# Four staging buffers for weight gradients, and a new order and new buffer addresses, in a gated S4-plus-MLP forward and backward kernel

## The chip, the cores and the metric

The kernel runs on one core of one Trainium2 chip, in one launch. The metric is device time in microseconds (us), the median of several runs. Inputs and all outputs are bf16.

## The reference

A gate mixes two branches; the kernel computes the result and the gradients with respect to everything but the MLP's own input `x`, which is the same array as `u` and is not differentiated as such. L = 2048 rows, D = 448 channels, N = 256 states, F = 1792 hidden units.

```python
g = sigmoid((u * gate_w).sum(-1, keepdims=True))
# branch a: a state-space layer, as a long convolution through FFTs of length 2L
dt = exp(log_dt); A, B, C complex of D x N
K = einsum("dn,dnl,dn->dl", C, exp(dt*A*l), dt*B).real      # l = 0..L-1
a = irfft(rfft(pad(u)) * rfft(pad(K)))[:L] + u * Dskip
# branch b: an MLP with a squared ReLU
b = relu(x @ w1 + b1)**2 @ w2 + b2
y = g * a + (1 - g) * b
# outputs: y, and vjp(grad_out) for u, A, B, C (real and imaginary parts),
# log_dt, Dskip, w1, b1, w2, b2, gate_w       -> 15 outputs
```

## The kernel before

**How the program is made.** `build()` (from L618) records 2757 tasks: a matmul group with its shared bank, a vector or scalar operation, a DMA. A task has an engine and often an alternative (a cast on ACT or DVE, a DMA issued by SP or POOL). Nothing is scheduled when the kernel is built: `replay` (L448) reads two tables of numbers. `ORDER` (L461) holds every task once, as its number times four plus the number of the alternative taken, in the order in which instructions are emitted; so it sets each engine's queue and which engine takes which task. `HOMES` (L580) gives the address of each of 808 buffers in one SBUF area, the "arena", of 106,368 bf16 elements per partition. Two buffers with one address take turns, and the later one's writer waits for the earlier one's last reader. Each engine runs its own queue in order; a DMA's issue instruction, too, waits at the head of its issuer's queue until its data and its target are free. All instructions are emitted in one loop, so the profile's lines tell only the kind: L1585 matmul, L1587 transpose on TensorE, L1589 transposing DMA, L1593 activation, L1595 cast, copy or DMA, L1597 any other element-wise operation. The names `arena` and `banks` stand for all of SBUF and PSUM (8 banks). DRAM scratch keeps its names: `sp` for spectra, `hd` for half-way results of inverse transforms, `br_d` for rows of the MLP branch, `st_d`, `pg_d`, `raw_d` for sums and tables of the parameter gradients, `dh_d` and `r2_d` for hidden activations.

**What it computes, in order of its ranks.**

- Head: loads, the gate, spectra of u and of g times the incoming gradient by two-step transforms (`fwd1` L750, `fwd2` L784) of matmuls with constant tables; the spectra go to `sp`.
- Dense branch: `x @ w1`, squared ReLU and `@ w2` in four blocks of rows, forward and backward. `project` (L975) makes the "dense rows" that the two row outputs need, and they wait in `br_d`. A column of matmuls over 16 row tiles forms each block of the gradient of w2 (L1060) and of w1 (L1270); ACT or DVE casts the bank into a staging buffer `dws`, and a DMA takes it to its output.
- State-space parameters in seven passes (L1134 to L1226): powers, tables, a first half that forms the convolution kernel, and a second half, the gradients, whose sums go to `st_d`.
- Last part (from L1297): the spectrum of the kernel K (`spk`); then, for each of two outputs and four quarters q, a saved spectrum is loaded (`sx`), DVE multiplies it (T1 and T2), `inv1` (L802) does the first step of the inverse transform, casts the banks into a buffer `st` and writes it to `hd` (`hd1` for y, `hd2` for the gradient of u). Then come the outputs' rows (L1374 for y, L1400 for the gradient of u): a quarter loads its part of `hd` (`hs`, 896 KB) and four pieces of dense rows (`brr`, from `br_d`), TensorE adds the dense rows to the second step of the inverse (`inv2` L1342), DVE or ACT moves the result out of the bank into a buffer `ao`, and four DMAs take the rows out.
- Parameter gradients: two groups (passes 0 to 3, then 4 to 6) of element-wise operations of DVE on `st_d`, `pg_d` and `raw_d` (L1434), the sum for log_dt (`dlog`), 36 transposes of 128x128 and 12 of 128x64, and the outputs of A, B and C.

**What holds the rows of one output together.** A load of `hs` reads, on every partition, pieces that all eight groups of `inv1` of that output have written; it waits for all writes of `hd1` (or `hd2`):

```python
d(hd[i], 8 * q * D, [[32 * D, 128], [1, 8 * D]], [("hd", i)])      # load_hs, L820: one key for the whole of hd[i]
```

Each quarter of y then is (L1374):

```python
hs = load_hs(1, q)
br = load_br(0, q)
st = R.buf("ao", 1792)
for hp in range(2):
    py = R.ps("y", 2)
    inv2(hs, hp, q, ..., [(negI..., br...)])
    for x in range(2):
        V("scalar_tensor_tensor", out=jk..., in0=ps..., in1=Gt..., accum_out=dg...)
        V("scalar_tensor_tensor", out=st..., in0=ps..., scalar=gt32..., in1=br...)
rows_out(o0, q, st)
```

The first of the two DVE operations gives the gate's gradient, which the rows of the gradient of u need; so every quarter of y comes ahead of any of the gradient of u.

Of the kernel before, what the change touches and what calls it, by code (L numbers as in the profile page):

```python
# [447 lines left out]
def replay(R, order, homes):  # L448
# [169 lines left out]
def build(nc, R, A_u, Ap, A_log_dt, A_Dskip, B_w1, B_b1, B_w2, B_b2, gate_w, grad_out, outs):  # L618
# [66 lines left out]
    place = {}  # L685
# [177 lines left out]
    for e in range(6):  # L863
        sg = R.buf("dks", 896)
# [193 lines left out]
    dws = [place[f"dws{i}"] for i in range(2)]  # L1058
    nd = 0
    for j in range(FT):  # L1060
# [4 lines left out]
        sg = dws[nd % 2]  # L1065
# [208 lines left out]
    for jg in range(4):  # L1274
# [6 lines left out]
        for dt in range(4):  # L1281
# [4 lines left out]
            sg = dws[nd % 2]  # L1286
# [341 lines left out]
```

## Time and profile before

| | |
|---|---|
| median of 3 runs | 805.7 us (802.41, 805.7, 806.49) |
| the profiled execution | 806.5 us, of which the span of instructions 804.7 us |
| mean granted TensorE clock | 0.904 of full speed |
| matmuls on PE | 11,044 |
| busy: PE, DVE, ACT, POOL | 662.0, 566.1, 476.8, 161.7 us |
| DMA bytes | 138.07 MB, mean 172 GB/s |
| tasks by engine: DVE, ACT, POOL, SP | 831, 713, 270, 164 |

A row of a stretch's table gives its start and end, its length, then for each engine the busy time and the number of instructions, then the granted clock, the mean busy share of the core's 16 DMA engines, and GB/s. A row of waits names the waiting engine and line, what it waited for, the total, how often, and the longest. A row of the timeline has start, length, engine, line, operation, shapes and count, and in brackets how long the engine had stood still before it and what came last. SP has no busy time of its own; it only issues DMAs.

### The profile page before, as it was taken

What the parts mean: (1) busy time and instruction counts of PE and PEld (TensorE: products, weight loads), DVE (VectorE), ACT (ScalarE), POOL (GpSimd) and SP (SyncE); (2) the same over time, 40 slices, a digit from 0 to 9 for tenths busy, and PEclk for the clock granted to TensorE, in tenths of its full rate; (3) what the DMA queues carried; (4) which work ended last, traced back from release to release, by engine and by line L of the source; (5) the groups of instructions that cost most, each with busy time, mean ns of one, the idle gap of its engine ahead of it and who ended that gap; (6) DMA issues with size and microseconds to landing.
All of it is one profiled execution on the core that took longest, in us unless ns stands there. A gap on an engine that the chain in (4) does not pass through costs nothing.

```text
span 804.7 us, 24883 instructions
## 1 busy us (share of the span) xinstructions
PE 662.0 (82%) x11046; PEld 445.2 (55%) x11046; DVE 566.1 (70%) x863; ACT 476.8 (59%) x711; POOL 161.7 (20%) x274
## 2 busy tenths in 40 slices
PE   4587899887999597797779999987698899677477
PEld 4575475556676465465477777765565545542112
DVE  4796766978589658858958895797442665786665
ACT  4999887789687576466555543632226966143125
POOL 6121321202102001210000221022001033332434
PEclk9869999999999899898789999989689999697759
DMA  9846968724206465553424553335942559997996
GB/s 297 253 174 222 339 243 316 197 94 163 73 37 190 150 135 126 126 90 80 136 44 100 185 184 111 101 96 180 174 136 97 108 175 259 236 223 245 263 314 190
DMA packets 112805, 138.07 MB, mean 172 GB/s; under 512 B 75701, under 2 KB 93674, under 8 KB 112058
## 3 DMA queue, kind: packets, MB, share of 16 engines
q0 software_dynamic: 20480, 78.95, 30.1%
q1 hardware_dynamic: 88922, 55.84, 28.5%
q10 hardware_dynamic: 3296, 1.70, 0.9%
q8 instruction: 86, 1.41, 0.7%
q14 instruction: 21, 0.17, 0.1%
HBM read 60.01 MB, written 60.16 MB: 149 GB/s over the span
## 4 chain that ended last, share of the span: by engine, by line
PE 50%; DVE 19%; ACT 10%; DMA 10%; issue 8%; POOL 1%; SPq 0%; ACTq 0%; DVEq 0%; POOLq 0%
PE banks L1585 50%; DVE arena L1597 16%; ACT arena L1595 8%; DVE arena L1595 4%; DMA arena<-br_d 3%; ACT arena L1593 2%; DMA arena<-in_A_u_dram 1%; DMA arena<-c_MI 1%; DMA hd<-arena 1%; DMA arena<-sp 1%; DMA arena<-in_grad_out_dram 1%; DMA out_dram<-arena 1%; DMA arena<-st_d 1%; POOL hd L1595 0%; ACT L1593 0%
## 5 line engine op out<-in xcount | busy, mean ns | idle before, releaser
L1585 PE MATMUL banks<-arena 128*128 128x128 bf16 (+10 forms) x10998 | 658.8, 251 | 138.0 <-ACT arena L1595 45.3
L1585 PEld LDWEIGHTS <-arena 128*32 128x32 bf16 (+6 forms) x10994 | 442.2, 104 | 349.4 <-issue 191.0
L1597 DVE TENSOR_TENSOR arena<-arena 128x256 bf16<-128x256 bf16 (+14 forms) x501 | 384.7, 812 | 66.5 <-ACT arena L1593 30.8
L1595 ACT CAST arena<-banks 128x896 bf16<-128x896 f32 (+6 forms) x411 | 314.1, 828 | 180.1 <-PE banks L1585 137.7
L1595 DVE CAST arena<-banks 128x1024 bf16<-128x1024 f32 (+6 forms) x73 | 75.5, 1048 | 95.4 <-PE banks L1585 92.0
L1593 ACT ACTIVATE arena<-arena 128x256 f32<-128x256 f32 (+8 forms) x138 | 77.5, 586 | 49.7 <-DVE arena L1597 25.0
L1595 POOL DMA_DIRECT2D out_dram<-arena x54 | 29.5, 548 | 170.8 <-ACT arena L1595 130.6
L1597 DVE TENSOR_TENSOR arena<-banks,arena 128x1024 bf16<-128x1024 f32 (+2 forms) x46 | 40.5, 891 | 26.4 <-PE banks L1585 16.6
L1595 ACT COPY arena<-banks 128x168 f32<-128x168 f32 (+3 forms) x36 | 15.3, 438 | 64.9 <-PE banks L1585 64.6
L1597 DVE SCALAR_TENSOR_TENSOR arena<-arena 128x128 f32<-128x128 f32 (+1 forms) x86 | 30.0, 349 | 13.3 <-DMA arena<-in_A_u_dram 9.9
L1595 POOL DMA_DIRECT2D hd<-arena x35 | 22.2, 635 | 61.6 <-ACT arena L1595 51.3
L1595 ACT COPY arena<-arena 128x256 bf16<-128x256 bf16 (+4 forms) x54 | 27.9, 564 | 8.4 <-DVE arena L1597 8.1
L1595 ACT CAST arena<-arena 128x768 bf16<-128x768 f32 (+3 forms) x33 | 26.5, 807 | 9.2 <-DVE arena L1597 9.2
L1597 DVE SCALAR_TENSOR_TENSOR arena<-banks,arena 128x448 bf16<-128x448 f32 x32 | 19.0, 647 | 17.1 <-PE banks L1585 17.1
L1593 ACT ACTIVATE arena<-banks 128x1024 bf16<-128x1024 f32 (+1 forms) x29 | 25.6, 904 | 7.6 <-PE banks L1585 7.4
L1595 POOL DMA_DIRECT2D br_d<-arena x24 | 13.3, 556 | 77.6 <-ACT arena L1595 72.4
L1595 POOL DMA_DIRECT2D st_d<-arena x11 | 6.1, 551 | 90.3 <-ACT arena L1595 90.3
L1595 POOL DMA_DIRECT2D r_d<-arena x14 | 11.6, 829 | 52.1 <-ACT arena L1593 36.3
L1597 DVE TENSOR_SCALAR arena<-arena 128x448 bf16<-128x448 bf16 (+9 forms) x50 | 17.6, 387 | 5.2 <-ACT arena L1593 1.9
L1595 POOL DMA_DIRECT2D dh_d<-arena x7 | 7.8, 1108 | 55.0 <-DVE arena L1597 46.4
L1595 POOL DMA_DIRECT2D arena<-in_grad_out_dram x20 | 12.9, 648 | 14.9 <-PE banks L1585 11.7
L1595 POOL DMA_DIRECT2D arena<-br_d x21 | 11.2, 538 | 3.5 <-DMA hd<-arena 1.9
(48 smaller groups left out, 84.0 us busy)
## 6 DMA issues: line engine op xcount, KB each, us to landing
r_d<-arena POOLq DMA_DIRECT2D x14, 896.0 KB, 5.8
arena<-hd SPq DMA_DIRECT2D x12, 896.0 KB, 13.2
hd<-arena POOLq DMA_DIRECT2D x35, 224.0 KB, 5.1
dh_d<-arena POOLq DMA_DIRECT2D x7, 896.0 KB, 6.0
sp<-arena POOLq DMA_DIRECT2D x6, 896.0 KB, 9.1
arena<-r_d POOLq DMA_DIRECT2D x5, 896.0 KB, 5.1
arena<-sp SPq DMA_DIRECT2D x5, 896.0 KB, 8.7
out_dram<-arena POOLq DMA_DIRECT2D x28, 112.0 KB, 4.2
```

The lines of the kernel that those rows point to most:

```text
L1585: fn(out, **kw)
L1593: fn(out, kw.pop("in_"), kw.pop("func"), **kw)
L1595: fn(out, kw["in_"])
L1597: fn(out=out, **kw)
```

## The change

The code changes in four lines: two staging buffers become four. Everything else is in the two tables, which are new from the first row to the last.

```diff
-                  ("dws0", 512), ("dws1", 512), ("xu1", 1024), ...
+                  *((f"dws{i}", 512) for i in range(4)), ("xu1", 1024), ...
...
-    dws = [place[f"dws{i}"] for i in range(2)]
+    dws = [place[f"dws{i}"] for i in range(4)]
...
-        sg = dws[nd % 2]
+        sg = dws[nd % 4]
...
-            sg = dws[nd % 2]
+            sg = dws[nd % 4]
...
 ORDER = [
-    0, 10, 13, 4, 16, 22, 26, 28, 34, 40, 36, 44, 72, 48, 52, 56, 61, 65, 68, 1724, 1440, 292, 92, 1732,
+    0, 10, 13, 4, 21, 18, 26, 28, 34, 37, 41, 44, 72, 48, 57, 61, 69, 65, 52, 1440, 260, 92, 1732, 1724,
...
```

The tasks, their shapes and their number stay: 2757 tasks, 11,044 matmuls on PE. 307 tasks change their engine, most of them casts that ACT and DVE exchange: DVE has 834 tasks (831 before), ACT 710 (713), POOL 258 (270), SP 176 (164). Of the loads of dense rows, 13 go from POOL's queue to SP's and 5 the other way. By the addresses in `HOMES`, buffers of these names have so many different places:

| buffers | before | after |
|---|---|---|
| staging of weight gradients (`dws`) | 2 | 4 |
| dense rows for the outputs (`brr`, 8 loads) | 6 | 7 |
| rows that leave (`ao`, 8) | 5 | 7 |
| products of spectra (`T1`, 12) | 10 | 11 |
| loaded spectra (`sx`, 8) | 8 | 7 |
| loaded half-way results (`hs`, 8) | 8 | 7 |
| half-way results before they are written (`st`, 24) | 19 | 15 |
| first-step results of forward transforms (`b1`) | 23 | 21 |

Three places where the order differs. First SP's queue in the last part. `arena<-br_d 32x2x896` is one piece of dense rows, `arena<-hd 128x3584` a load of `hs`, `hd<-arena 64x4x448` a write of half-way results, `out_dram<-arena 128x256` an output of the A, B and C gradients, `arena<-sp` a saved spectrum. Before:

```order
L1595 DMA arena<-sp 128x3584
L1595 DMA arena<-hd 128x3584
L1595 DMA out_dram<-arena 128x256
L1595 DMA arena<-hd 128x3584
L1595 DMA arena<-br_d 32x2x896 x2
L1595 DMA arena<-hd 128x3584
L1595 DMA out_dram<-arena 64x256
L1595 DMA out_dram<-arena 128x256
L1595 DMA hd<-arena 64x4x448
L1595 DMA out_dram<-arena 32x2x896 x3
L1595 DMA arena<-br_d 32x2x896 x2
L1595 DMA arena<-hd 128x3584
```

After:

```order
L1595 DMA st_d<-arena 128x256 x2
L1595 DMA hd<-arena 64x4x448
L1595 DMA arena<-br_d 32x2x896 x4
L1595 DMA arena<-st_d 128x1536
L1595 DMA arena<-br_d 32x2x896 x4
L1595 DMA hd<-arena 64x4x448
L1595 DMA arena<-br_d 32x2x896
L1595 DMA hd<-arena 64x4x448
L1595 DMA arena<-hd 128x3584 x3
L1595 DMA out_dram<-arena 128x256 x2
L1595 DMA arena<-hd 128x3584
```

Nine pieces of dense rows and the second group's load of `st_d` now stand ahead of the first load of `hs`; before, loads of `hs` and dense rows alternated and writes of `hd2` stood between them. The first three loads of `hs` now follow the last writes of `hd1`, and the fourth stands behind two outputs.

Second, DVE's queue where the last rows and the second group of parameter gradients meet. `SCALAR_TENSOR_TENSOR 128x448` is an operation of y; `TENSOR_TENSOR 128x384` and `128x3x4x16` are operations of the second group; `COPY 128x768` empties a bank of transposes; the rows of `128x2x2` are the gate's gradient. Before:

```order
L1597 SCALAR_TENSOR_TENSOR arena<-banks,arena 128x448 x16
L1595 CAST arena<-arena 128x2x2 x2
L1597 TENSOR_TENSOR arena<-arena 128x2x2 x2
L1595 CAST arena<-arena 128x2x2 x2
L1597 TENSOR_TENSOR arena<-arena 128x384 x2
L1597 TENSOR_TENSOR arena<-arena 128x3x4x16 x2
L1597 TENSOR_TENSOR arena<-arena 128x384 x3
```

After:

```order
L1597 TENSOR_TENSOR arena<-arena 128x3x4x16
L1597 TENSOR_TENSOR arena<-arena 128x384 x2
L1597 TENSOR_TENSOR arena<-arena 128x3x4x16 x2
L1597 SCALAR_TENSOR_TENSOR arena<-banks,arena 128x448 x2
L1597 TENSOR_TENSOR arena<-arena 128x384
L1597 SCALAR_TENSOR_TENSOR arena<-banks,arena 128x448
L1597 TENSOR_TENSOR arena<-arena 128x384
L1597 SCALAR_TENSOR_TENSOR arena<-banks,arena 128x448
L1597 TENSOR_TENSOR arena<-arena 128x384 x3
L1595 COPY arena<-banks 128x768
L1597 TENSOR_TENSOR arena<-arena 128x384 x2
L1597 SCALAR_TENSOR_TENSOR arena<-banks,arena 128x448 x9
```

Before, the second group began after the last operation of y. Now most of the group (27 operations) stands ahead of the first operation of y, the rest of it between them, and 9 operations of y come last.

Third, ACT's queue at the last blocks of the gradient of w1. `CAST 128x512`, `65x512`, `128x256` are casts into `dws` (512 or 256 columns of w1's gradient); `CAST 128x896` belongs to the inverse transforms, `128x672` to the gradient passes. Before:

```order
L1595 CAST arena<-banks 128x512
L1593 ACTIVATE arena<-arena 128x4x4x16
L1595 CAST arena<-banks 128x896 x4
L1595 CAST arena<-banks 65x512
L1595 CAST arena<-banks 128x256 x2
L1595 CAST arena<-banks 128x896 x8
L1595 CAST arena<-banks 128x256
```

After:

```order
L1595 CAST arena<-banks 65x512
L1595 CAST arena<-banks 128x896
L1595 CAST arena<-banks 128x256
L1595 CAST arena<-banks 128x896 x3
L1595 CAST arena<-banks 128x672 x2
L1595 CAST arena<-banks 128x256
L1595 CAST arena<-banks 128x672
L1595 CAST arena<-banks 128x256
```

The last casts into `dws` come earlier than most of the casts of the inverse transforms, spread between casts of the gradient passes, and each has a buffer that was last used four casts before, not two.

More of the change, by code (lines that the diff above doesn't have):

```diff
@@ L686, in build @@
     for nm, n in (("dKc", 4704), ("dKg0", 672), ("dKg1", 672), ("stg0", 512), ("stg1", 512), ("Z0", 5376), ("Z1", 5376), *((f"YT{i}", 2048) for i in range(NYT)), ("KS", NA * 112), ("KT0", 336), ("KT1", 336),
-                  ("dws0", 512), ("dws1", 512), ("xu1", 1024), ("dnC", 7168), ("xT0", 1024), ("xT1", 1024), ("br0", 448), ("br1", 448),
+                  *((f"dws{i}", 512) for i in range(4)), ("xu1", 1024), ("dnC", 7168), ("xT0", 1024), ("xT1", 1024), ("br0", 448), ("br1", 448),
                   *((f"XP{i}", 5376) for i in range(NXP)), ("Y", 8192), ("X1", 5376), ("Vt", 4096), ("xu0", 1024), ("ry", 2560), ("rx", 3072), ("X0", 5376), ("dnB", FT * D), ("dnA", 7200)):
```

296 rows, old and new, of tables (HOMES, ORDER) are left out of this document.

## The prediction

> **What bounds the kernel now.** I read the profile's page first.
>
> ```profile
> span 804.7 us, 24883 instructions
> PE 662.0 (82%) x11046; PEld 445.2 (55%) x11046; DVE 566.1 (70%) x863; ACT 476.8 (59%) x711; POOL 161.7 (20%) x274
> PE   4587899887999597797779999987698899677477
> PEclk9869999999999899898789999989689999697759
> ```
>
> PE works 662.0 of 804.7 us, so it is the bound on average, and the change leaves its matmuls as they are. What can change is the 142.7 us in which PE stands. Slices of the page show them: the head, then small gaps, then the last six slices, where PE is at 4 to 7 tenths and its clock falls. The table of stretches splits it (columns: start, end, length, busy time and count of PE, PEld, DVE, ACT, POOL, granted clock, share of the DMA engines, GB/s).
>
> ```profile
> 140.00:640.00 500.00, 427.18 (x8678) 307.18 (x8670) 359.56 (x522) 291.89 (x454) 67.08 (x103) 0.92 0.47 125
> 660.00:700.00 40.00, 32.88 (x449) 20.41 (x448) 24.86 (x15) 17.10 (x26) 12.30 (x22) 0.89 0.98 267
> 700.00:740.00 40.00, 29.75 (x223) 16.33 (x222) 32.75 (x39) 13.69 (x19) 11.99 (x20) 0.80 1.01 240
> 740.00:805.00 65.00, 41.23 (x281) 13.49 (x277) 39.63 (x104) 21.42 (x36) 26.93 (x49) 0.74 0.78 239
> 752.70:783.30 30.60, 16.47 (x85) 3.52 (x89) 18.09 (x55) 6.42 (x14) 10.37 (x20) 0.50 0.95 290
> ```
>
> In the long middle PE stands 500 − 427.18 = 72.8 us with the DMA engines half used. After 700 it stands 105 − 29.75 − 41.23 = 34.0 us, and no engine is full there but the DMAs. So I read waits of two stretches, 640 to 805 and 140 to 640 (engine, line, what it waited for, total, times, longest).
>
> ```profile
> PE banks L1585 <- DMA arena<-br_d: 21.9, 5, 9.6
> PE banks L1585 <- ACT arena L1595: 7.9, 3, 5.7
> ACT arena L1595 <- DMA out_dram<-arena: 8.1, 2, 6.6
> ...
> PE banks L1585 <- ACT arena L1595: 22.5, 29, 3.8
> PE banks L1585 <- DVE arena L1597: 21.6, 13, 5.4
> ```
>
> Three rows are the last part, two the middle. The timeline gives the places in the last part.
>
> ```profile
> 725.20 0.37 ACT L1595 CAST arena<-banks 128x256 bf16<-128x256 f32 x1 [6.60 <-DMA out_dram<-arena]
> 725.62 6.65 PE L1585 MATMUL banks<-arena 128*128 128x256 bf16 x44 [5.73 <-ACT arena L1595]
> 736.70 5.65 PE L1585 MATMUL banks<-arena 128*128 128x448 bf16 x29 [4.43 <-DMA arena<-br_d]
> 758.96 3.50 PE L1585 MATMUL banks<-arena 128*128 128x448 bf16 x20 [9.64 <-DMA arena<-br_d]
> 767.60 3.50 PE L1585 MATMUL banks<-arena 128*128 128x448 bf16 x20 [5.14 <-DMA arena<-br_d]
> ```
>
> The first two are one event: ACT may not cast w1's gradient before a staging buffer has been read out, and PE waits for the bank. The other three are quarters of y, and what came last for each is dense rows, not `hs`. The chain that ended last goes through both (start, length):
>
> ```profile
> 717.30 7.74 DMA out_dram<-arena
> ...
> 727.01 9.55 DMA arena<-br_d
> ...
> 749.65 4.71 DMA hd<-arena
> ...
> 756.01 11.46 DMA arena<-br_d
> ...
> 796.68 3.32 PE banks L1585 x4
> 800.07 0.52 ACT arena L1595
> ```
>
> **Part by part.** All sums are made against the profiled execution's own 806.5 us; the median of the runs is 0.8 less, far under the 0.5% (4 us) that a measurement of this kernel can tell from no change.
>
> *Staging.* With four buffers a cast waits for the write-out four casts before. The chain's 7.74 us of write-out at 717.30 goes, and PE's wait of 5.73 with it. Bounds: 0, if the bank was freed late for another reason, and −8.1, all that ACT waits for such writes here. I take −5.7, the row of the place itself. Next late there is DVE's products, which have 32.75 of 40 us busy.
>
> *Dense rows.* In the order before, a piece of `br_d` that a y needs stands on SP behind a load of `hs`, which waits for `hd`; after, nine stand ahead of the first `hs`. The three waits, 4.43 + 9.64 + 5.14 = 19.2, go. Bounds 0 and −21.9 (all five). I take −19.2, since those rows have the order's places.
>
> *A new wait.* In the order after, the last writes of `hd1` stand directly ahead of the first loads of `hs`, and the y that need them follow on PE with little else left: the transforms of the gradient of u are done by then. Rows for that chain, from the last cast of an inverse transform:
>
> ```profile
> L1595 ACT CAST arena<-banks 128x896 bf16<-128x896 f32 x46 | 39.9, 911 | 23.3 <-PE banks L1585 18.6 <-DMA arena<-br_d 2.8 <-DMA out_dram<-arena 1.5
> L1595 POOL DMA_DIRECT2D hd<-arena x27 | 17.0, 633 | 44.8 <-ACT arena L1595 38.5 <-DMA arena<-sp 4.1 <-DMA hd<-arena 1.8
> 651.96 8.21 DMA arena<-sp
> arena<-hd SPq DMA_DIRECT2D x8, 896.0 KB, 13.6
> hd<-arena POOLq DMA_DIRECT2D x27, 224.0 KB, 4.9
> L1587 PE MATMUL banks<-arena 128*128 128x128 bf16 x36 | 2.9, 220 | 0.0
> L1587 PE MATMUL banks<-arena 128*64 128x128 bf16 x12 | 1.0, 223 | 0.0
> ```
>
> Cast 0.9, issue 0.6, write 4.7 (the chain's row), load 8.2 (a load of the same 896 KB that the chain of the stretch from 640 waited for, from `sp`): +14.4. Below: transposes of the parameter gradients fill it, 2.9 + 1.0 = 3.9, so +10.5. Above: write 4.9 and load 13.6, the medians, and the same cast and issue: +20.0. I take 14.4, since nothing else is left to be loaded at that moment if dense rows came earlier. Behind the waiting load on SP stand two outputs and all later `hs`; y's DVE operations and then those of the gradient of u wait for it.
>
> *DVE's second group.* 27 operations of it now stand ahead of the first y on DVE.
>
> ```profile
> L1597 DVE TENSOR_TENSOR arena<-arena 128x384 f32<-128x384 f32 x19 | 10.1, 561 | 2.5 <-DMA arena<-st_d 2.3
> L1597 DVE TENSOR_TENSOR arena<-arena 128x192 bf16<-128x192 f32 x10 | 4.5, 497 | 0.1
> L1597 DVE SCALAR_TENSOR_TENSOR arena<-banks,arena 128x448 bf16<-128x448 f32 x32 | 19.0, 647 | 17.1 <-PE banks L1585 17.1
> ```
>
> About 18 × 0.561 + 9 × 0.497 = 14.6 us, as long as the new wait of 14.4, which covers them. What costs is a late start: +2, an estimate near the covered end; bounds 0 and +7.3, if half of them lie bare.
>
> *Later loads of hs.* The fourth stands on SP behind two outputs that wait for transposes and their copies; the nearest wait of that kind is PE's longest for ACT in this stretch, 5.7. Bounds 0 and +5.7, I take +3, the middle, as the three loads ahead give PE work meanwhile.
>
> *The end.* Before, the last chain was the sum for log_dt, 3.32 + 0.52 after the last group of DVE. Now the rows of the gradient of u are last. Bounds 0 and −3.8, I take −2, as their cast and writes then stand at the end.
>
> *The middle.* 307 tasks change engines and all are re-ordered; no row says which way PE's 22.5 + 21.6 = 44.1 us of waits for ACT and DVE go. A quarter of them, 11, in either direction is my bound, and 0 my value. With it go the other places (one more of six for `brr`, two more of five for `ao`), whose waits I find in no row of PE, and the fewer places for half-way results, which cost nothing as long as POOL's writes keep pace. In the last of the gradient passes PE now has its big group, S, later and takes the inverse transforms first; this only exchanges work.
>
> Sum: −5.7 − 19.2 + 14.4 + 2 + 3 − 2 + 0 = −7.5; 806.5 − 7.5 = **799.0**. Its own range: the distances to the near bounds, without the middle and with dense rows staying in effect, added as independent. Downwards 2.4, 2.7, 3.9, 2, 3, 1.8 give 6.7, so 792; upwards 5.7, 5.6, 5.3, 2.7, 2 give 10.2, so 809.
>
> *A rule against the dense rows' term.* The rows of stretches after 660 show the DMA engines at 0.98, 1.01 and 0.78, and one issue of a dense row on POOL costs what this row says:
>
> ```profile
> L1595 POOL DMA_DIRECT2D arena<-br_d x21 | 11.2, 538 | 3.5 <-DMA hd<-arena 1.9 <-issue 1.2 <-DVE arena L1597 0.4
> arena<-br_d POOLq DMA_DIRECT2D x21, 112.0 KB, 7.3
> arena<-br_d SPq DMA_DIRECT2D x11, 112.0 KB, 9.7
> ```
>
> A move of 13 issues away from POOL is worth 13 × 0.538 = 7.0 us in itself. I take the larger 19.2 because the loads are also issued earlier, not only elsewhere, and the wait is mostly in the queue: the piece that PE wanted at 767.60 was issued at 756.01, behind the write at 749.65. The Trainium skill, "DMA: Bandwidth & Descriptors", section "Issuing engines are not separate DMA queues", says that DMAs of all issuing engines run on the same 16 engines and that spreading them saves only the issue time. The landings of 7.3 and 9.7 us by POOL and SP agree that SP is no faster road.
>
> *The clock.* After its wait of 9.64 us PE runs at 0.50 for 30.6 us (752.70 to 783.30), with 16.47 us of work, half of which, 8.2, is the most a full clock could give. I count nothing: a new wait of 14.4 would bring the same low clock, and that stretch ends with loads. The Trainium skill, "TensorE: Matmul & The Clock Gate", section "HAM oscillation — how this bites in real kernels", puts the limit at idle gaps of about 3.4 us, after which work starts throttled; by it the low clock stays after the new wait, and the sum stays at 799.0.
>
> **The rivals.**
>
> *The middle gains.* The search found places there too: PE loses a quarter of its 44.1 us of waits, 799.0 − 11 = 788. For it: DVE and ACT have 0.72 and 0.58 busy there, so the waits are of order, not of amount. Against: the pools there are no bigger.
>
> *The middle loses 11:* 810. Against: the counts by engine hardly move.
>
> *The DMA engines bound the end.* 0.98 × 40 + 1.01 × 40 + 0.78 × 65 = 130 of 145 us after 660 are busy. Then neither the dense rows' earlier issue nor the new wait counts, both being waits for the same bytes: 806.5 − 5.7 + 2 + 3 − 2 = 803.8. Against: 0.78 at the end leaves 14 us.
>
> *Only issue time is saved:* dense rows give 7.0 instead of 19.2, and the rest stays: 811.2. For it speak landings of 11.46 us; it is the way of the rule on issuing engines, above.
>
> *The change doesn't do what it says:* by addresses, `hs`, `sx`, `st` and `b1` have fewer places, not more; new waits for them eat the 7.5: 806.5.
>
> *Slower: the loads of hs set the pace of all rows of y.* All four now come after the last write of `hd1`, one end to everything. A quarter of y takes DVE 8 × 0.647 = 5.2 us; if the loads land one after another at their median of 13.6, each of two more quarters waits 13.6 − 5.2 = 8.4. The new waits are then 20.0 + 2 × 8.4 = 36.8 against the 24.9 saved: 806.5 + 11.9 = 818.4. It decides from the point where an `hs` takes over 5.2 us more than the last. Against: 896 KB at the 290 GB/s of 752.70 to 783.30 take 3.1 us.
>
> **How the numbers follow.** Forecast 0.37 (0.30 of it below 802.5, 0.07 within 4 us of 806.5), middle gains 0.17, middle loses 0.04, DMA engines bound 0.11, issue time alone 0.06, not as it says 0.03, loads of hs 0.22. Faster by over 0.5%: 0.30 + 0.17 = 0.47. Within 0.5%: 0.07 + 0.04 + 0.11 + 0.03 = 0.25. Slower: 0.06 + 0.22 = 0.28. Cases of both signs hold much, so the range goes from 783 (the middle's gain with 5 more from the near bounds of staging and dense rows, 2.4 + 2.7) to 818, about the middle of the slower rival; half of that, 0.11, and some 0.05 below lie outside.
>
> **What would show it.** In the profile after: no wait of ACT's 128x256 casts for out_dram; no wait of PE for br_d of over 4 us; one wait of PE for `arena<-hd` of 10 to 20 us ahead of the first y, with DVE in its second group meanwhile; the last instructions casts and writes of the gradient of u. I am wrong if PE's stand before the first y is over 25 us or comes again at the later quarters (slower rival), if waits for br_d remain at landings over 9 us with full DMA engines (DMA rivals), or if PE's busy time from 140 to 640 is off 427 by over 8 at the same work.

## The result and the profile after

The kernel after takes 793.5 us (median of 4 runs, 792.28 to 795.33), the kernel before 804.9 us beside it: a ratio of 0.9863, 95% interval 0.9829 to 0.9897, or 11 us less (8 to 14). A second timing gave 0.9857 (0.9797 to 0.9917). The forecast was 799.0, in a range of 783 to 818, with 0.47 on faster by over 0.5%.

The profiled execution after has 792.28 us, with a span 14.2 us shorter than before's. The page's rows:

```profile
span 790.5 us, 24859 instructions
PE 649.5 (82%) x11046; PEld 437.3 (55%) x11046; DVE 570.6 (72%) x866; ACT 472.8 (60%) x708; POOL 154.5 (20%) x262
PE   4678898969999789688887998798398889975577
PEclk9878999989999899999999999999799999999558
```

PE stands as long as before (790.5 − 649.5 = 141.0 us against 142.7); its busy time is 12.5 us less, for the same matmuls at a higher granted clock. That tells no cause: the rows don't say whether the clock is higher because PE stands at other times, or the other way round. The stretches (columns as before):

```profile
140.00:640.00 500.00, 425.93 (x8730) 300.16 (x8726) 347.69 (x510) 280.29 (x445) 58.84 (x93) 0.95 0.48 130
660.00:700.00 40.00, 39.47 (x532) 22.80 (x530) 36.62 (x34) 26.85 (x40) 16.80 (x28) 1.00 0.88 268
700.00:740.00 40.00, 19.95 (x220) 13.45 (x218) 38.56 (x50) 14.39 (x20) 18.99 (x33) 0.86 0.95 304
740.00:790.50 50.50, 38.32 (x231) 11.24 (x223) 28.84 (x78) 14.71 (x26) 19.68 (x37) 0.70 0.81 257
```

From 660 to 700 PE is full, where it had 32.88 of 40 us (over 640 to 700 it is 56.74 against 52.84). From 700 to 740 it is DVE that is full, 38.56 of 40 (32.75 before), and PE has less than before. PE's waits from 640 on:

```profile
PE banks L1587 <- DVE arena L1597: 12.2, 2, 11.6
PE banks L1585 <- DVE arena L1597: 11.5, 9, 2.1
PE banks L1585 <- DMA arena<-hd: 2.6, 2, 1.9
PE banks L1585 <- ACT arena L1595: 2.5, 5, 1.3
...
PE banks L1585 <- DMA arena<-br_d: 0.4, 1, 0.4
```

The 21.9 us of waits for dense rows are gone, and so is the 5.73 for a staged cast. In their place stands one wait of 11.6 us, not for `hs` as forecast, but for DVE, at a transpose of the parameter gradients (L1587). The timeline shows why (PE, then DVE):

```profile
735.99 0.29 PE L1587 MATMUL banks<-arena 128*128 128x128 bf16 x1 [11.61 <-DVE arena L1597]
...
739.63 2.66 PE L1585 MATMUL banks<-arena 64*32 64x448 bf16 x18 [0.68 <-DMA arena<-hd]
```

```profile
711.74 11.30 DVE L1597 TENSOR_TENSOR arena<-arena 128x3584 bf16<-128x3584 bf16 x10 [0.47 <-DMA arena<-sp]
722.95 0.26 DVE L1597 TENSOR_SCALAR arena<-arena 128x384 bf16<-128x384 bf16 x1
723.12 8.11 DVE L1597 TENSOR_TENSOR arena<-arena 128x512 f32<-128x512 f32 x14
731.67 10.04 DVE L1597 TENSOR_TENSOR arena<-arena 128x384 f32<-128x384 bf16 x20 [0.45 <-ACT arena L1593]
741.64 1.26 DVE L1597 SCALAR_TENSOR_TENSOR arena<-banks,arena 128x448 bf16<-128x448 f32 x2
```

PE has done its last inverse transform at 724 and has nothing but transposes and y left. `hs` is there at 739.6; until 741.6 DVE works with gaps of under half a us, the end of the products, the rest of the first group (`128x512`), then the second (`128x384`). In the kernel before, that second group was what came last on DVE, after all of y:

```profile
777.02 3.61 DVE L1597 TENSOR_TENSOR arena<-arena 128x384 f32<-128x384 f32 x7 [2.30 <-DMA arena<-st_d]
...
781.70 10.59 DVE L1597 TENSOR_TENSOR arena<-arena 128x384 f32<-128x384 bf16 x21 [0.18 <-ACT arena L1593]
```

So the theory to test was: **the gain of the last part is the second group's 20 us, moved from behind y into the wait for `hs`.** The rivals: it is the dense rows' order (19.2 by the prediction), the staging (5.7), or the middle, where the granted clock rose from 0.92 to 0.95.

### The profile page after: what moved, and what is told of

The parts are those of the page before. It is cut to its first block, busy times and chain, and to the rows that moved or that the text cites. A ratio compares the mean times of both kernels' runs of the same rounds, so it can differ in the third digit from the quotient of the medians.

```text
span 790.5 us, 24859 instructions
## 1 busy us (share of the span) xinstructions
PE 649.5 (82%) x11046; PEld 437.3 (55%) x11046; DVE 570.6 (72%) x866; ACT 472.8 (60%) x708; POOL 154.5 (20%) x262
## 4 chain that ended last, share of the span: by engine, by line
PE 52%; DVE 18%; DMA 11%; ACT 10%; issue 7%; POOL 1%; ACTq 0%; SPq 0%; DVEq 0%; POOLq 0%
PE banks L1585 52%; DVE arena L1597 16%; ACT arena L1595 7%; DMA arena<-in_grad_out_dram 4%; DMA arena<-hd 3%; DVE arena L1595 2%; ACT arena L1593 2%; DMA hd<-arena 2%; DMA arena<-in_A_u_dram 1%; DMA arena<-br_d 1%; DMA arena<-in_B_w_dram 1%; ACT L1593 0%; POOL hd L1595 0%; POOL arena L1595 0%; ACTq L1595 0%
## 5 line engine op out<-in xcount | busy, mean ns | idle before, releaser
L1585 PE MATMUL banks<-arena 128*32 128x42 bf16 (+10 forms) x10998 | 643.9, 250 | 123.6 <-DVE arena L1597 39.6
L1585 PEld LDWEIGHTS <-arena 128*32 128x32 bf16 (+5 forms) x10994 | 432.4, 103 | 331.3 <-issue 180.2
L1597 DVE TENSOR_TENSOR arena<-arena 128x256 bf16<-128x256 bf16 (+13 forms) x502 | 385.7, 814 | 47.5 <-ACT arena L1593 25.1
L1595 ACT CAST arena<-banks 128x896 bf16<-128x896 f32 (+4 forms) x411 | 313.9, 827 | 165.3 <-PE banks L1585 138.9
L1595 DVE CAST arena<-banks 128x1024 bf16<-128x1024 f32 (+5 forms) x73 | 74.9, 1040 | 86.6 <-PE banks L1585 73.7
L1593 ACT ACTIVATE arena<-arena 128x256 f32<-128x256 f32 (+7 forms) x136 | 76.2, 583 | 48.9 <-DVE arena L1597 28.3
L1595 POOL DMA_DIRECT2D out_dram<-arena x60 | 32.5, 544 | 178.4 <-ACT arena L1595 98.9
L1597 DVE TENSOR_TENSOR arena<-banks,arena 128x1024 bf16<-128x1024 f32 (+2 forms) x46 | 40.5, 891 | 30.3 <-PE banks L1585 16.6
L1597 DVE SCALAR_TENSOR_TENSOR arena<-arena 128x128 f32<-128x128 f32 (+1 forms) x86 | 30.2, 351 | 16.3 <-DMA arena<-in_A_u_dram 10.5
L1595 ACT CAST arena<-arena 128x768 bf16<-128x768 f32 (+3 forms) x28 | 21.8, 789 | 9.9 <-DVE arena L1597 9.9
L1597 DVE SCALAR_TENSOR_TENSOR arena<-banks,arena 128x448 bf16<-128x448 f32 x32 | 19.8, 649 | 5.7 <-PE banks L1585 3.1
L1595 POOL DMA_DIRECT2D r_d<-arena x14 | 11.6, 825 | 61.7 <-ACT arena L1593 46.5
L1597 DVE TENSOR_SCALAR arena<-arena 128x448 bf16<-128x448 bf16 (+9 forms) x51 | 18.3, 394 | 6.9 <-PE banks L1585 5.1
L1595 POOL DMA_DIRECT2D dh_d<-arena x5 | 5.5, 1109 | 59.3 <-DVE arena L1597 44.4
L1587 PE MATMUL banks<-arena 128*128 128x128 bf16 (+1 forms) x48 | 5.8, 305 | 12.2 <-DVE arena L1597 12.2
```

What stands on the lines that cost most here:

```text
L1585: fn(out, **kw)
L1587: fn(out, kw["in_"], kw["ident"], **({"tile_position": kw["tile_position"]} if "tile_position" in kw else {}))
L1593: fn(out, kw.pop("in_"), kw.pop("func"), **kw)
L1595: fn(out, kw["in_"])
L1597: fn(out=out, **kw)
```

## The experiments

Each was timed in five rounds beside the kernel before; ratios are to that. The first three start from the kernel before, and take one reason of the prediction each.

**Dense rows early, on the kernel before.**

```diff
 # SP's queue
+DMA arena<-br_d x14
 DMA arena<-hd
 DMA out_dram<-arena
 DMA arena<-hd
-DMA arena<-br_d x2
 DMA arena<-hd
...
```

> The kernel before, with one thing changed: the 14 issues of dense rows (br_d) for the four quarters of y that stood behind the first load of hs now stand ahead of it on SP, and the buffers of the third and fourth quarter have addresses of their own that are free by then. If the waits of PE for br_d are a matter of queue order, as the prediction has it, the rows 4.43, 9.64 and 5.14 go and the time falls by 12 to 19 us (ratio 0.977 to 0.985; less than the sum where the loads of hs land right behind). If the DMA engines bound the last part, the same bytes are only moved: PE waits for hs in place of br_d, and the time stays within 4 us (0.995 to 1.005). If only issue time counts, about 7 us go (0.991).

Measured: 0.9948 (0.9917 to 0.998), 4 us. PE's waits from 640 on:

```profile
PE banks L1585 <- DVE arena L1597: 13.4, 6, 4.4
PE banks L1585 <- DMA arena<-hd: 6.2, 2, 4.7
PE banks L1585 <- ACT arena L1595: 6.1, 3, 4.0
PE banks L1585 <- DMA arena<-br_d: 5.2, 2, 3.2
```

Waits for `br_d` fall from 21.9 to 5.2, as queue order predicts, but 7.3 come back as waits for DVE and 6.2 for `hs`. What remains is near the price of the issue time alone (9 fewer issues on POOL at 0.538 us, 4.8). The prediction weighed that price, and took the row of waits.

**Two more staging buffers for the last block of w1's gradient, on the kernel before.**

```diff
+    late = [R.buf(f"dwx{i}", 512) for i in range(2)]
...
-            sg = dws[nd % 2]
+            sg = late[dt] if jg == 3 and dt < 2 else dws[nd % 2]
```

> The kernel before, with two more staging buffers for the last block of w1's gradient alone (its first two pieces), so that no cast there waits for a write-out two casts before; order untouched. By the prediction's term ACT's wait of 6.60 and PE's of 5.73 at 725 go and the time falls by 4 to 6 us (0.993 to 0.995). The rival: the wait was covered, the loads of hs and br_d behind it come no earlier, and PE stands longer at the first y instead: within 2 us (0.998 to 1.002).

Measured: 1.0027 (0.9996 to 1.0057): nothing gained. One line was added, so the emission has other numbers here (L1586 and L1598 for L1585 and L1597):

```profile
PE banks L1586 <- DMA arena<-br_d: 20.0, 4, 9.9
PE banks L1586 <- DVE arena L1598: 12.2, 4, 4.5
PE banks L1586 <- ACT arena L1596: 2.6, 3, 1.9
```

ACT's part of PE's waits fell from 7.9 to 2.6 and DVE's rose from 6.1 to 12.2. The wait was covered.

**Both.**

> The two edits together on the kernel before: dense rows ahead of the loads of hs, and two more staging buffers for the last block of w1's gradient. If the terms add, 17 to 25 us (0.969 to 0.979), which would be more than the whole change gave, since its new wait isn't in it. If the tail is bound by something behind both (DMA engines, or DVE's products and y), it gives no more than the better of the two alone.

Measured: 0.9949 (0.992 to 0.9977), no more than the dense rows alone. With y done, DVE stands for the second group's data, as in the kernel before, and then has that group to do alone:

```profile
759.10 0.29 DVE L1596 CAST arena<-arena 128x4 f32<-128x4 bf16 x2
763.00 3.61 DVE L1598 TENSOR_TENSOR arena<-arena 128x384 f32<-128x384 f32 x7 [3.61 <-DMA arena<-st_d]
```

**Two staging buffers, on the kernel after.** The casts take turns in the order in which they stand; three write-outs that stood behind the next use of their buffer come ahead of it.

```diff
-    dws = [place[f"dws{i}"] for i in range(4)]
+    dws = [place[f"dws{i}"] for i in range(2)]
...
-            sg = dws[nd % 4]
+            sg = dws[int("010010110101101001010100111001"[nd])]
```

> The kernel after with two staging buffers instead of four, used in turn in the order in which the casts stand; three write-outs that stood behind the next use of their buffer are issued just ahead of it. If four buffers carry the staging term in the new order, 3 to 6 us of it come back (ratio to before 0.990 to 0.994, after was 0.986). The rival: in the new order the casts stand far enough apart, and it is the order, not the number of buffers, that removed the wait: 0.985 to 0.988.

Measured: 0.9991 (0.9959 to 1.0024). All of the change's gain is lost, 10 us by the difference to 0.9863, where 3 to 6 had been expected. A wait for a write-out is back in the profile:

```profile
711.60 2.70 ACT L1595 CAST arena<-banks 128x256 bf16<-128x256 f32 x5 [9.53 <-DMA out_dram<-arena]
...
712.92 6.61 PE L1585 MATMUL banks<-arena 64*128 64x448 bf16 x66 [6.04 <-ACT arena L1595]
```

ACT stands 9.53 us for a write-out. Up to there PE ran 7.4 us behind the profile after, from there on it is 14 to 16 behind. The 7.4 had come by 642, where ACT's rows name only 2.2 us of such waits; the profiled execution (807.4 us) is also the slowest of the twelve, whose median is 800.5. So the step at 711 belongs to the buffers, and the 7.4 before it stays open. The buffers carry the new order: worth nothing in the old one, they are worth most of the gain in this one, whose last casts stand close together.

**The kernel after again**, beside the next three.

> The kernel after, unchanged, timed beside the others of this group. 0.983 to 0.990 of before.

Measured: 0.9857 (0.9797 to 0.9917).

**The second group late, on the kernel after.**

```diff
 # DVE's queue
-TENSOR_TENSOR 128x384 ... (second group)
 SCALAR_TENSOR_TENSOR 128x448 ... (y)
+TENSOR_TENSOR 128x384 ... (second group)
 # PE, ACT, SP, POOL: the group's transposes, copies and outputs at the very end
```

> The kernel after with one thing undone: DVE's second group of parameter gradients, the transposes that need it and the sum for log_dt stand behind the last operation of y again, as before; two operations of DVE behind it go to ACT, and eleven buffers whose lives got longer have other addresses, last used long before. Theory: the new order gains in the last part because DVE does this group while y waits for hs, and is then full to the end. Then y's operations start when hs lands (739.6 in the profile after, 2 us earlier than now) and end some 8 us earlier, but 20 us of the group follow them with their transposes and outputs: 4 to 9 us slower than after (0.991 to 0.998 of before). Rival: the order of the loads alone makes the gain, and where the group stands is free: within 3 us of after.

Measured: 1.0143 (1.009 to 1.0196), 23 us slower than after by the ratios.

```profile
736.62 3.52 PE L1585 MATMUL banks<-arena 64*32 64x448 bf16 x20 [11.01 <-DMA arena<-hd]
744.68 2.66 PE L1585 MATMUL banks<-arena 64*32 64x448 bf16 x18 [4.55 <-DMA arena<-hd]
...
786.29 8.68 PE L1585 MATMUL banks<-arena 128*128 128x448 bf16 x40 [9.32 <-ACT arena L1595]
```

```profile
785.34 0.91 ACT L1595 CAST arena<-banks 128x896 bf16<-128x896 f32 x1 [11.20 <-DVE arena L1597]
```

```profile
737.30 1.27 DVE L1597 SCALAR_TENSOR_TENSOR arena<-banks,arena 128x448 bf16<-128x448 f32 x2 [12.14 <-PE banks L1585]
...
772.02 13.82 DVE L1597 TENSOR_TENSOR arena<-arena 128x384 f32<-128x384 bf16 x27 [0.45 <-ACT arena L1593]
```

Here the forecast's new wait lies bare: PE stands 11.01 us for `hs`, DVE 12.14, and 4.55 follow at the second quarter. Y ends at 766.6 instead of 772.9, and the group follows it. The 9.32 at 786 belongs to the edit, not to the group's place as such. PE waits there for ACT's cast at 785.34, and that cast waits 11.20 us for DVE: by `HOMES` its target, an `ao` of the gradient of u (address 103,248, 1792 elements), shares addresses with a temporary of the second group (104,320), which this order uses late. Without it some 14 us would remain (an estimate, 23 − 9.3); the size was expected as 4 to 9, the sign is clear.

**The second group's data early, on the run of both edits.**

```diff
 # SP's queue
 DMA arena<-br_d x14
+DMA st_d<-arena
 DMA arena<-hd
 DMA out_dram<-arena
 DMA arena<-hd x2
+DMA arena<-st_d 128x1536
...
-DMA arena<-st_d 128x1536
```

> The kernel before with dense rows ahead of the loads of hs and two staging buffers more, as in the run of both edits, and besides: the last write of st_d goes out on SP ahead of the first load of hs instead of late in POOL's queue, and the second group's load of st_d stands behind the third load of hs. In the run of both edits DVE stood from 758 to 763 for that load, with all of y done. If DVE's work is what the end waits for, 4 to 5 us go (0.988 to 0.990 of before). Rival: the rows of the gradient of u are late behind it anyway: 0.994 to 0.996 as without it.

Measured: 0.9871 (0.9818 to 0.9923), as fast as the kernel after within what these runs tell apart.

```profile
759.41 0.29 DVE L1596 CAST arena<-arena 128x4 f32<-128x4 bf16 x2
759.61 3.61 DVE L1598 TENSOR_TENSOR arena<-arena 128x384 f32<-128x384 f32 x7
```

DVE's pause after y is gone. Sixteen moved DMA issues and two buffers, in the old order of everything else, give what the change gave. The second group still runs behind y here.

**A cross: the order of after to about 660 us, then that of before.** The rest needs new addresses for 58 of 91 buffers.

> A cross of the two: the order, engines and four staging buffers of after up to about 660 us, then the rest in the order and on the engines of before; 58 of 91 buffers that begin in the rest have new addresses, so some waits for memory may be new. By PE's work done in the two profiles, after is 6 us ahead at 640. If that belongs to the order of the middle, this kernel is 6 us faster than before or more (0.988 to 0.994). If it is the scatter of one profiled run, it isn't faster than before (0.998 to 1.008), and all of the change's gain lies in the last part.

Measured: 1.014 (1.008 to 1.02). It decides nothing, since the seam costs time that neither kernel has: from 640 to 700 PE has 44.79 of 60 us in place of 56.74 in the profile after. Whether the middle gains is looked at below, from the work that PE has done by 640.

```profile
640.00:700.00 60.00, 44.79 (x589) 25.55 (x588) 34.65 (x24) 35.59 (x46) 11.86 (x19) 0.91 0.47 126
```

**Dense rows late, on the kernel after.**

```diff
 # SP's queue
-DMA arena<-br_d x4
 DMA arena<-st_d 128x1536
-DMA arena<-br_d x4
+DMA arena<-br_d
 DMA hd<-arena
-DMA arena<-br_d
 DMA hd<-arena
 DMA arena<-hd
+DMA arena<-br_d x3
 DMA arena<-hd x2
 DMA out_dram<-arena x2
 DMA arena<-hd
+DMA arena<-br_d x5
```

> The kernel after with SP's eight pieces of dense rows for three quarters of y put back behind loads of hs: three behind the first, five behind the one of the second y. Prediction's term: PE's waits for br_d come back, by the rows of before 4 to 10 us each; pieces are then issued at 736 and 741 in place of 715 to 727 and land 5 to 7 us later, so y starts at 743 to 748 in place of 740: 4 to 9 us slower than after (0.991 to 0.997 of before). Rival: DVE is busy with its second group until 748 and covers it: within 2 us of after (0.984 to 0.989).

Measured: 0.9926 (0.9891 to 0.9961), about 5 us slower than after. PE's first y moves to 743.83, and two waits return:

```profile
743.83 3.49 PE L1585 MATMUL banks<-arena 128*128 128x448 bf16 x20 [3.41 <-DMA arena<-br_d]
...
754.83 5.44 PE L1585 MATMUL banks<-arena 128*128 128x448 bf16 x15 [3.85 <-DMA arena<-br_d]
```

So in both orders the place of the dense rows is worth 4 to 5 us.

**All loads of hs for y together, on the kernel after.**

```diff
 # SP's queue
-DMA arena<-hd x3
+DMA arena<-hd x6
 DMA out_dram<-arena x2
-DMA arena<-hd
...
-DMA arena<-hd
...
-DMA arena<-hd
```

> The kernel after with one change of SP's order: the other three loads of hs for y stand directly behind the first, ahead of two loads for the gradient of u and of the outputs of the A, B and C gradients; six buffers have other addresses. Prediction's term for the later loads was +3 (0 to 5.7). In the profile after, DVE stood 2.46 and 1.98 us at the second y behind such a load. If the term is real, 2 to 5 us less than after (0.979 to 0.984 of before). Rival: more loads at once land later, and the first y starts later by as much: within 2 us of after.

Measured: 0.9889 (0.9841 to 0.9936), no gain, though PE's waits for `hs` fall from 2.6 to 0.2 us. Of the two waits of DVE that were to go, the one of 2.46 was not a load's: by its row in the profile after it ended with a write-out (`DMA out_dram<-arena`). From 720 to 770 the median from issue to landing rose from 7.7 to 11.5 us (after first, this run second):

```profile
arena<-hd SPq DMA_DIRECT2D x8, 896.0 KB, 7.7
```

```profile
arena<-hd SPq DMA_DIRECT2D x8, 896.0 KB, 11.5
```

**The last quarter's hs early, on the run with the second group's data early.** Its load moves up on SP, ahead of two write-outs of w1's gradient and three of y.

> The kernel before with dense rows ahead of the loads of hs, two staging buffers more and the second group's load early, and besides the load of hs for the last quarter of y some 7 us earlier on SP, ahead of two write-outs of w1's gradient. In the run without it DVE stood 3.29 us at that quarter and PE 4.45. If DVE's queue is what the end waits for, 3 us less than without it (0.982 to 0.985 of before). Rival: the gradient of u, whose loads keep their place, sets the end: as without it (0.986 to 0.989).

Measured: 0.9864 (0.9805 to 0.9923), the same within the interval. DVE's pause at that quarter is gone, but in this profile a spectrum that had come in time before came late:

```profile
712.15 4.56 DVE L1598 TENSOR_TENSOR arena<-arena 128x3584 bf16<-128x3584 bf16 x3 [11.13 <-DMA arena<-sp]
```

**That spectrum's load earlier too.** On POOL it moves ahead of two write-outs and two loads of the incoming gradient.

> The kernel before with all moves so far (dense rows ahead of hs, two staging buffers more, the second group's load early, the last quarter's hs early) and one more: the load of the second spectrum of the gradient of u goes out on POOL ahead of four other issues, some 7 us earlier. In the profile without it DVE stood 11.13 us for that load, which the run without the early hs had not shown (3.05). If that wait is what took the gain of the early hs, the time comes to 0.979 to 0.984 of before, below the kernel after. Rival: the load waits for the DMA engines, not in the queue, and the early hs is worth nothing: 0.985 to 0.990.

Measured: 0.9851 (0.981 to 0.9891), 791.5 us. DVE's waits for spectra fall from 13.4 to 3.9 us, but the first y waits 4.63 for its `hs`, where it waited 2.16 in the run with the second group's data early:

```profile
735.84 11.39 PE L1586 MATMUL banks<-arena 64*32 64x448 bf16 x81 [4.63 <-DMA arena<-hd]
```

The row doesn't say why; the moved load of the last quarter's `hs` goes out only at 739.5, after this wait. The run's ratio is the lowest of all, and not told apart from the kernel after (0.9863).

## Why the prediction was right, and where its steps were not

The sign, the rough size (−7.5 against −11) and the place of the new wait were right. Most of the terms were wrong in size, and their errors cancelled: that the sum came so near is luck.

- **Dense rows, −19.2: the largest miss.** The step that failed is "I take −19.2, since those rows have the order's places". The waits went as said, 21.9 to 0.4; the time did not follow. Alone they gave 4 us, and undone in the new order they cost 5. A wait named in a row is the last of several; DVE and `hs` were close behind. The Trainium skill, "DMA: Bandwidth & Descriptors", section "Issuing engines are not separate DMA queues", which the prediction weighed against its term, puts the gain of spreading issues at the issue time; the 4.8 us of nine issues agree in size with the 4 measured. That agreement proves nothing, though: the run with the dense rows late left every issue on its engine, and still cost 5 us.
- **Staging, −5.7.** In the old order it gave nothing; "next late there is DVE's products" was said, and not priced. In the new order two buffers in place of four cost 10 us. The term is a condition of the order, not a gain by itself.
- **The new wait, +14.4.** The run with the group late shows its place and length: 11.01 us bare, inside the bounds of 10.5 and 20.0 and under the 14.4 taken; the 4.55 at the second quarter belong to the term of the later loads. In the kernel after it costs little, since DVE needs until 741.6 in any case and `hs` is there at 739.6. Then the wait isn't a term to add to DVE's.
- **DVE's second group, +2, and the end, −2.** These were the mis-sized steps on the other side. Before, the group ran from 777.0 to 796.5, behind the last y; the prediction saw only the 3.8 us of the sum for log_dt behind it go. In fact most of 20 us left the end, and the group's place is worth some 14 to 23 us in the new order. So the theory holds for the new order; as the one cause of the gain it does not, since the run with the second group's data early gains as much with the group behind y. Undoing one of the three (group, buffers, dense rows) costs 23 (some 14 without the shared buffer), 10 and 5 us, together far over the gain of 11: they depend on each other, and are no shares of it. What the group's move alone brings in the old order was not run.
- **Later loads of hs, +3.** Moving the loads up returned nothing; with six issued in a row in place of three, the median landing went from 7.7 to 11.5 us.
- **The middle, 0.** In seven profiles with before's middle the granted clock from 140 to 640 is 0.92 to 0.94, in six with after's middle and four buffers 0.95 to 0.96, at the same busy time of 423 to 428 us. That looks like a gain: busy time times clock is some 395 against 404 us. But this product doesn't measure work to 9 us. Over the whole kernel it gives 598 us before (662.0 × 0.904) and 603 after (649.5 × 0.929), for the same matmuls. Another estimate counts the matmuls that have begun by 640, each at the mean distance to the next one of its form in stretches with a full clock, from these traces: 494 to 499 us of work are done in the seven profiles, 492 to 497 in the six, the cross among them. So no lead of after's middle is shown, and the rival of the middle gains no support. By 700 after's order is ahead, with 548 to 552 (five profiles) against 539 to 543, and by 740 no longer, with 566 to 567 against 562 to 568. How much of the higher clock is due to four staging buffers (0.93 with two) stays open.
- **The rivals.** PE's wait before the first y is one, and stays under 15 us, so loads of `hs` don't set the pace; that the DMA engines bound the end is not borne out either: the same bytes end 10 us sooner in the run with the second group's data early.
- **The clock.** After the wait of 11.61 us the page has two slices of 20 us at 5 tenths; before, after the wait of 9.64, it has one. The Trainium skill, "TensorE: Matmul & The Clock Gate", section "HAM oscillation — how this bites in real kernels", says that work after idle gaps of over about 3.4 us starts throttled; the trace agrees. The prediction counted nothing for the clock there; the stretch from 740 to the end has 0.70, where it had 0.74.

## What to carry to other kernels

Add up waits of one chain only: rows that name 19 us of waits are worth what the next resource leaves of them, here 4 to 5. When a tail has one engine with work that depends on nothing late, look where that work stands before looking at the waits; moved into a wait it no longer adds to the end. A buffer count and an order are one decision: two more buffers gave nothing in the old order, and the new order gave nothing without them. And when an edit makes work late, look which addresses it shares: some 9 of the 23 us of one run above came from a shared buffer.

## What the runs showed beside

One and the same load of a spectrum, 896 KB, can land 10 us apart in two runs of nearly the same order: in the profile with the second group's data early it was there within 15 us of its issue (683.7, used at 698.9), in the one with the last quarter's `hs` early, with the same instructions ahead of it, DVE got it 25 us after its issue (686.5, used at 712.2). From 680 to 715 the table of stretches gives the DMA engines a share of 1.01 in the one and 1.15 in the other (the table's share can pass 1), with 224 and 167 GB/s; there a lead of 15 us was no safe one.
